# Attention feeding a gated FFN on one core: one small-tile phase per slot, outputs two slots behind, V loaded by ScalarE, nine pairs turned by TensorE

## The chip, the cores and the metric

The kernel runs on one core of a Trainium2 chip. The metric is the time of one execution on the device in microseconds (us); lower is better. The time of the kernel before is the median of three runs. The profile comes from one execution more.

The core has five engines that run side by side, each in its own order: TensorE (PE; its weight loads are listed as PEld), VectorE (DVE), ScalarE (ACT), GpSimd (POOL) and SyncE (SP), which here only starts transfers. TensorE writes only to PSUM. Transfers run on 16 DMA engines that all queues share.

## The reference

`q`, `k` and `v` are 8 x 8 x 576 x 64 (batch, heads, sequence, head dimension), 32-bit floats. Two attentions are added and fed to a gated FFN:

```
q_d, k_d, v_d = means of q, k, v over groups of 4 positions        # 144 positions
out_up    = repeat(softmax(q_d k_d^T / 8) v_d, 4)                  # pooled attention
out_local = softmax(q k^T / 8 where |i - j| < 4) v                 # local attention
x = (out_up + out_local), heads side by side                       # 4608 x 512
out = (relu(x w_gate) * (x w_val)) w_out                           # 512 -> 1536 -> 512
```

## The kernel before

**Pairs and slots.** Two heads of one batch make a pair; there are 32 pairs, and four pairs give 576 rows of `x`. Pair `p` is loaded into `qst`, `kst` and `vst` (three buffers each, `load_qk` L134 and `load_v` L154, all from SP's queue; V takes four transfers), cast to 16 bits (`cast_q`, `cast_k`, `cast_v`), and q and k are turned so that the head dimension is on partitions. Pairs below `N_PE` = 6 are turned by TensorE (`turn_pe`, L215), which also gives the means of q and k in `pd`; the others are turned by two DMA transposes on SP (`turn_dma`, L246), and GpSimd makes their means (`pool_qk`, L258: `ptq`, `pd`, `ptk`, `pd`).

**Attention of a pair.** `scores` (L276) puts on TensorE the means of V (8 matmuls with `p32`, L281), the pooled scores (L292) and the local scores (48 small matmuls, L305), all into the PSUM tile `at` (four banks). `maxima` masks the local scores, takes maxima on VectorE and subtracts on GpSimd (`dd`, L336). `exps` (L343) is on ScalarE: four exponentials of the pooled scores (`e_d`, L348), one of the local ones (`ee`, L356), and the copy of V's means (`vd16`, L357). `weigh` (L359) takes reciprocals on VectorE, scales on GpSimd (`e_d` L365, `pp` L368) and turns the pooled weights by a DMA transpose (`adT`, L374). `turn_p` (L380) turns the local weights on VectorE (`pT`). `sums` (L386) multiplies the weights with V on TensorE (local L391, pooled L401), copies the pooled result to `odx` on ScalarE (L411), and adds both into `xT` on VectorE (L416).

**FFN.** `xT` is cut into nine chunks of 512 tokens. An h unit (`unit_h`, L429) is eight matmuls of 512 columns (L434) into two PSUM buffers, a ReLU on ScalarE (L443) and a product on VectorE (`gT`, L444). A y unit (`unit_y`, L446) is 12 such matmuls (L449) into one PSUM buffer and a copy on ScalarE (L458); `store_y` sends the rows out. Four PSUM buffers serve both kinds. There are 108 h units and 36 y units in the fixed order of `units` (L468): 12 h units of chunk 0, then for each chunk c its 12 h units with a y unit of chunk c - 1 behind the second, fifth, eighth and eleventh.

**Order.** The schedule is written by hand: each engine runs its instructions in the order in which the program issues them, and the build adds the waits between engines. A head (L486 to L526) does the attention of pairs 0 to 3 and loads the weights in pieces from GpSimd's queue. Then each pass of the loop at L530, a slot, does the scores of pair s, some FFN units (`ffn(a[0])` to `ffn(a[3])`; 12 in all in slots 4 to 8, four a slot from slot 9 on), and the sums of pair s - 1. What is left of `units` runs after the loop. Within a slot the order is: loads of pair s + 3, means of pair s + 1 (`pool_qk`), scores and maxima, `ffn(a[0])`, `exps`, `weigh`, `ffn(a[1])`, `sums(s - 1)`, casts of k and `turn_dma` of pair s + 2, `ffn(a[2])`, `turn_p`, `ffn(a[3])`.

Of the kernel before, what the change touches and what calls it, by code (L numbers as in the profile page):

```python
# [16 lines left out]
N_PE = 6  # L17
# [43 lines left out]
def kernel(  # L61
# [39 lines left out]
    qst = many(3, [96, 2, 6, 64], FP32, "qst")  # L101
    kst = many(3, [96, 2, 2, 256], FP32, "kst")
    vst = many(3, [128, 2, 6, 64], FP32, "vst")
# [6 lines left out]
    adT = many(2, [128, 2, 2, 2, 80], FP16, "adT")  # L110
# [7 lines left out]
    vw = many(4, [128, 2, 6, 64], FP16, "vw")  # L118
    vd16 = many(2, [128, 2, 128], FP16, "vd16")
# [8 lines left out]
    pT = many(2, [128, 12, 32], FP16, "pT")  # L128
# [5 lines left out]
    def load_qk(p):  # L134
        base = 2 * p * S * D
        nc.sync.dma_start(qst[p % 3], _dap(q, base, [[D, 96], [S * D, 2], [96 * D, 6], [1, D]]))

        st = kst[p % 3].rearrange("p h c e -> p (h c) e")
# [14 lines left out]

    def load_v(p):  # L154
        st = vst[p % 3].rearrange("p h n d -> p (h n) d")
        for g in range(4):
# [4 lines left out]
            if p == 0 and g == 0:  # L161
                lo = 4
                nc.sync.dma_start(
                    d[0:4, 1:12, :], _dap(v, o + 96 * D, [[D, 4], [96 * D, 11], [1, D]])
                )
            if p == NP - 1 and g == 3:
                hi = 28
                nc.sync.dma_start(
                    d[28:32, 0:11, :], _dap(v, o + 28 * D, [[D, 4], [96 * D, 11], [1, D]])
                )  # L170
            nc.sync.dma_start(
                d[lo:hi], _dap(v, o + lo * D, [[D, hi - lo], [96 * D, 12], [1, D]])
            )

    def load(p):
        load_qk(p)
        load_v(p)
# [20 lines left out]
    def cast_q(p, eng):  # L198
        copy(
            eng,  # L200
            q16[p % 2].rearrange("p j (h d) -> p j h d", d=D),
            qst[p % 3].rearrange("p h j d -> p j h d"),
        )

    def cast_k(p, c, eng):
# [3 lines left out]
            kst[p % 3][0:74, :, c, :].rearrange("p h (r d) -> p r h d", d=D),  # L209
        )  # L210

    def cast_v(p, eng):
        copy(eng, vw[p % 4], vst[p % 3])
# [44 lines left out]
    def pool_qk(p):  # L258
# [4 lines left out]
        )  # L263
        kg = kT[p % 3]
# [10 lines left out]

    def scores(p):  # L276
        qt, kt, pdt, vt = qT[p % 3], kT[p % 3], pd[p % 3], vw[p % 4]
        for n in range(8):
            m = n if n < 6 else n - 2
            x, kc = n % 4, n // 4  # L280
            nc.tensor.matmul(  # L281
                out=at[32 * x : 32 * x + 32, kc, 288:416],
                lhsT=p32,
                rhs=vt[:, :, m, :],
                start=True,
                stop=True,
                tile_position=(0, 32 * x),
            )
        for c in range(2):
            for h in range(2):  # L290
                lo = 64 * h
                nc.tensor.matmul(  # L292
                    out=at[0:72, h, 144 * c : 144 * c + 144],
# [6 lines left out]
        for n in range(6):  # L300
            for g in range(4):
                c, m = n // 3, 4 * (n % 3) + g
                for h in range(2):
                    lo = 64 * h
                    nc.tensor.matmul(  # L305
                        out=at[32 * g : 32 * g + 32, 2 + h, 32 * n : 32 * n + 32],
# [6 lines left out]

    def maxima(p):
        c = col[p % 2]
        nc.vector.tensor_tensor(  # L318
            out=sm[p % 2].rearrange("p (h n) j -> p h (n j)", h=2),
            in0=at[:, 2:4, 0:192],  # L320
            in1=_sap(mask, (0, 128), 0, [[0, 2], [1, 192]]),
            op=ALU.add,
        )
        nc.vector.tensor_reduce(  # L324
            out=c[0:72, 36:40].rearrange("p (h c) -> p h c", h=2),
            in_=at[0:72, 0:2, 0:288].rearrange("p h (c j) -> p h c j", c=2),
# [8 lines left out]
        nc.vector.tensor_reduce(out=c[:, 0:12], in_=sm[p % 2], axis=AX.X, op=ALU.max)  # L335
# [3 lines left out]
            in1=_sap(c, (0, 128), 0, [[1, 12], [0, 32]]),  # L339
# [3 lines left out]
    def exps(p):  # L343
        c = col[p % 2]
        for h in range(2):
            for cc in range(2):
                hc = 2 * h + cc
                nc.scalar.activation(  # L348
                    out=e_d[p % 2][0:72, h, cc, 0:6, 0:24],
                    in_=at[0:72, h, 144 * cc : 144 * cc + 144].rearrange("p (n j) -> p n j", j=24),  # L350
# [4 lines left out]
                )  # L355
        nc.scalar.activation(out=ee[p % 2], in_=dd[p % 2], func=AF.Exp, scale=scale)  # L356
        nc.scalar.copy(out=vd16[p % 2], in_=at[:, 0:2, 288:416])  # L357

    def weigh(p):  # L359
        c = col[p % 2]  # L360
        nc.vector.reciprocal(out=c[0:72, 48:52], in_=c[0:72, 44:48])  # L361
        nc.vector.tensor_reduce(out=c[:, 12:24], in_=ee[p % 2], axis=AX.X, op=ALU.add)  # L362
        nc.vector.reciprocal(out=c[:, 24:36], in_=c[:, 12:24])  # L363
# [3 lines left out]
        )  # L367
        nc.gpsimd.tensor_tensor(  # L368
# [5 lines left out]
        nc.sync.dma_start(  # L374
            adT[p % 2].rearrange("p h c k g -> p (h c k) g"),
            e_d[p % 2].rearrange("p h c n j -> p (h c n j)"),
            transpose=True,
        )

    def turn_p(p):  # L380
        nc.vector.transpose(
            pT[p % 2].rearrange("p n i -> p (n i)"), pp[p % 2].rearrange("p n j -> p (n j)")
        )


    def sums(p):  # L386
        vt, w, vd, ad = vw[p % 4], pT[p % 2], vd16[p % 2], adT[p % 2]
        for n in range(6):
            for h in range(2):
                for g in range(4):  # L390
                    nc.tensor.matmul(  # L391
                        out=at[64 * h : 64 * h + 64, g, 24 * n : 24 * n + 24],
                        lhsT=vt[32 * g : 32 * g + 32, h, n, :],
                        rhs=w[32 * g : 32 * g + 32, 6 * h + n, 0:24],
                        start=True,
                        stop=True,
                        tile_position=(32 * g, 64 * h),
                    )
        for kc in range(2):
            for h in range(2):  # L400
                nc.tensor.matmul(  # L401
                    out=at[64 * h : 64 * h + 64, 3, 144:288],
                    lhsT=vd[:, kc, 64 * h : 64 * h + 64],
                    rhs=ad[:, h, :, kc, 0:72],
                    start=(kc == 0),
                    stop=(kc == 1),
                    tile_position=(0, 64 * h),
                    skip_group_check=True,
                )
# [3 lines left out]
            in_=at[:, 3, 144:288].rearrange("p (n g m) -> p g n m", g=4, n=6),  # L413
        )
        b, kk = p // 4, p % 4
# [4 lines left out]
            in0=at[:, :, 0:144].rearrange("p g (n m f) -> p g n m f", n=6, f=4),  # L420
# [47 lines left out]
    units = []  # L468
    for c in range(NCH):
        for j in range(NJ):  # L470
            units.append(("h", c, j))
            if c and j % 3 == 1:
                units.append(("y", c - 1, j // 3))
# [12 lines left out]
    nc.sync.dma_start(eye, eye_dr)  # L486
    for t in kst[0], vst[0]:
        nc.gpsimd.memset(t, 0.0)
    load(0)
    nc.scalar.dma_start(p32, p32_dr)  # L490
    nc.scalar.dma_start(mask, mask_dr)
    for t in k16 + e_d:
        nc.vector.memset(t, 0.0)
    load(1)
    load(2)
    for t in qT:
        nc.gpsimd.memset(t[:, S:], 0.0)

# [5 lines left out]

    cast_early(0)
    turn_pe(0)
    w_at = {1: [0], 2: [1], 3: [2, 3]}

    for s in range(4):
        cast_early(s + 1)  # L510
        scores(s)
        maxima(s)
        turn_pe(s + 1)
        exps(s)
        weigh(s)
        for i in w_at.get(s, ()):
            load_w(moe_w_gate, wg, 384 * i, 384 * i + 384)
            load_w(moe_w_val, wv, 384 * i, 384 * i + 384)
        load(s + 3)
        turn_p(s)  # L520
        if s:
            sums(s - 1)
    sums(3)
    load_wo(0, 4)
    load_wo(4, 8)
    load_wo(8, 12)  # L526


    per_slot = {4: (1, 1, 1, 0), 5: (1, 1, 1, 0), 6: (1, 1, 0, 0), 7: (1, 1, 0, 0), 8: (1, 1, 0, 0)}
    for s in range(4, NP + 1):  # L530
        a = per_slot.get(s, (1, 1, 1, 1))
        if s == 4:
            cast_q(5, "act")
            cast_k(5, 0, "act")
            cast_k(5, 1, "act")
            cast_v(5, "dve")
        if s + 3 < NP and s > 3:
            load(s + 3)
        store_y()
        if s < NP:  # L540
            if s + 1 < NP and s + 1 >= N_PE:
                pool_qk(s + 1)
            if s + 2 < NP:
                cast_q(s + 2, "act")
            scores(s)
            maxima(s)
        ffn(a[0])
        if s + 1 < N_PE:
            turn_pe(s + 1)
        if s < NP:  # L550
            exps(s)
            if s + 2 < NP:
                cast_v(s + 2, "dve")
            weigh(s)
        ffn(a[1])
        if s > 4:
            sums(s - 1)
        if s + 2 < NP:
            cast_k(s + 2, 0, "act")
            cast_k(s + 2, 1, "act")  # L560
            turn_dma(s + 2)
        ffn(a[2])
        if s < NP:
            turn_p(s)
# [34 lines left out]
```

## Time and profile before

| | |
|---|---|
| median of 3 runs | 440.06 us (439.37 to 444.82) |
| profiled execution, its own time | 442.51 us |
| its span, first to last instruction | 440.8 us |
| TensorE busy | 368.5 us, 84% |
| VectorE, ScalarE, GpSimd busy | 225.9, 220.1, 164.0 us |
| mean granted TensorE clock | 0.969 |
| DMA traffic | 60.94 MB, mean 138 GB/s |

The page of the profile gives each engine's busy time; the span in 40 slices, each digit the busy share in tenths (PEclk is the clock that TensorE was granted, in tenths of full speed); the chain of work that ended last; groups of instructions by line; and the DMA queues. The trace behind it can be listed in order of time (start, length, engine, line, operation, out<-in, and in brackets the idle time before and what ended it) or summed over chosen stretches. SPq and ACTq are the queues from which SP and ScalarE start transfers. Where several instructions of a line are merged, "x48" is their number.

### The profile page before, as it was taken

Reading aid. Unit: us, or ns where it says so; the run is one execution under the profiler, and the core shown is the slowest. Engines: PE = TensorE matmul, PEld = TensorE weight load, DVE = VectorE, ACT = ScalarE, POOL = GpSimd, SP = SyncE. Lnnn points to the kernel's source line nnn. Section 1 sums busy time; section 2 is a strip of 40 time slices with the busy share of each in tenths; the row PEclk is TensorE's granted clock in tenths of the full one; section 3 lists DMA queues with packets and bytes.
Section 4 is the critical chain, followed back from the end, with each engine's and each line's share of the span. In section 5 each row is a group of like instructions: output and inputs, shape, how many; then the busy total and the mean of one; then the engine's idle time right before and its main releaser. Section 6 shows DMA issues by size and latency. Waiting matters only on the chain.

```text
span 440.8 us, 12346 instructions
## 1 busy us (share of the span) xinstructions
PE 368.5 (84%) x5048; PEld 181.1 (41%) x5048; DVE 225.9 (51%) x443; ACT 220.1 (50%) x595; POOL 164.0 (37%) x225
## 2 busy tenths in 40 slices
PE   1634049586789999999999999999979999999996
PEld 1433024243334445444444444444434444444442
DVE  2565024375546666666656666666645632223120
ACT  2464026454546666665666566666645423233321
POOL 2456401444564545544445545555444300000000
PEclk9999996788899999999999999999998999999999
DMA  9999999998999999999998899999654221010012
GB/s 159 158 176 192 180 204 194 153 137 153 154 154 174 175 170 183 188 165 168 164 183 171 184 160 176 186 177 185 134 113 70 42 40 48 26 48 24 25 48 95
DMA packets 165604, 60.94 MB, mean 138 GB/s; under 512 B 144940, under 2 KB 160940, under 8 KB 165548
## 3 DMA queue, kind: packets, MB, share of 16 engines
q1 hardware_dynamic: 159452, 55.34, 72.7%
q0 software_dynamic: 5808, 4.72, 7.6%
q8 instruction: 39, 0.64, 0.6%
q10 hardware_dynamic: 288, 0.11, 0.1%
q14 instruction: 17, 0.14, 0.1%
HBM read 42.08 MB, written 9.44 MB: 117 GB/s over the span
## 4 chain that ended last, share of the span: by engine, by line
PE 54%; ACT 12%; DVE 10%; DMA 10%; POOL 6%; issue 5%; SPq 2%; POOLq 0%; DVEq 0%; ACTq 0%
PE h_ps L434 22%; PE y_ps L449 21%; ACT e_d L348 7%; DMA kst<-in_k_dram 5%; DMA qst<-in_q_dram 4%; DVE col L324 4%; PE at L391 3%; PE at L305 3%; DVE sm L318 3%; ACT ee L356 3%; ACT vd L357 2%; DVE col L331 1%; PE at L401 1%; POOL dd L336 1%; PE at L292 1%
## 5 line engine op out<-in xcount | busy, mean ns | idle before, releaser
L444 DVE TENSOR_TENSOR gT<-r,h_ps 128x512 f16<-128x512 f16 x108 | 73.9, 685 | 131.0 <-PE h_ps L434 126.6
L434 PE MATMUL h_ps<-xT,wg 128*128 128x512 f16 x432 | 117.6, 397 | 0.0
L434 PE MATMUL h_ps<-xT,wv 128*128 128x512 f16 x432 | 115.9, 392 | 0.0
L443 ACT ACTIVATE r<-h_ps 128x512 f16<-128x512 f32 x108 | 64.7, 599 | 74.5 <-PE h_ps L434 74.5
L449 PE MATMUL y_ps<-wo,gT 128*128 128x512 f16 x432 | 100.0, 383 | 0.0
L434 PEld LDWEIGHTS <-wv 128*128 128x128 f16 x432 | 43.6, 101 | 55.2 <-issue 7.4
L434 PEld LDWEIGHTS <-wg 128*128 128x128 f16 x432 | 41.2, 101 | 49.5 <-issue 7.0
L449 PEld LDWEIGHTS <-gT 128*128 128x128 f16 x432 | 40.6, 98 | 48.8 <-issue 1.8
L260 POOL TENSOR_TENSOR ptq<-qT 128x288 f32<-128x288 f16 x26 | 17.3, 666 | 103.5 <-DMA qT<-q 94.7
L458 ACT COPY y_sb<-y_ps 128x512 f32<-128x512 f32 x36 | 21.1, 586 | 69.1 <-PE y_ps L449 69.1
L348 ACT ACTIVATE e_d<-at,col 72x144 f16<-72x144 f32 x128 | 46.6, 371 | 2.5 <-DVE col L331 1.9
L365 POOL TENSOR_TENSOR e_d<-e_d,col 72x576 f16<-72x576 f16 x32 | 36.6, 1142 | 24.9 <-DVE col L361 13.7
L391 PE MATMUL at<-pT,vw 32*64 32x24 f16 x1536 | 17.4, 188 | 31.6 <-ACT vd L357 30.1
L336 POOL TENSOR_TENSOR dd<-sm,col 128x384 f32<-128x384 f32 x32 | 27.0, 842 | 32.1 <-DVE col L335 31.9
L391 PEld LDWEIGHTS <-vw 32*64 32x64 f16 x1536 | 17.5, 108 | 43.0 <-issue 33.6
L192 ACT CAST q<-qst 96x768 f16<-96x768 f32 x32 | 26.3, 823 | 12.9 <-DMA qst<-in_q_dram 12.9
L416 DVE TENSOR_TENSOR xT<-at,odx 128x576 f16<-128x576 f32 x32 | 24.1, 754 | 14.2 <-ACT odx L411 14.2
L192 ACT CAST k<-kst 74x512 f16<-74x512 f32 x54 | 30.7, 618 | 0.0
L362 DVE TENSOR_REDUCE col<-ee 128x12 f32<-128x384 f16 x32 | 17.7, 552 | 19.3 <-ACT ee L356 19.2
L368 POOL TENSOR_TENSOR pp<-ee,col 128x384 f16<-128x384 f16 x32 | 26.5, 829 | 2.4 <-DVE col L363 2.2
L348 ACT ACTIVATION_READ_ACCUMULATOR e_d<-at,col 72x1 f32 x128 | 25.0, 196 | 0.0
L356 ACT ACTIVATE ee<-dd 128x384 f16<-128x384 f32 x32 | 16.6, 520 | 15.4 <-POOL dd L336 15.4
(47 smaller groups left out, 317.1 us busy)
## 6 DMA issues: line engine op xcount, KB each, us to landing
vst<-in_v_dram SPq DMA_DIRECT2D x126, 96.0 KB, 4.8
kst<-in_k_dram SPq DMA_DIRECT2D x30, 320.0 KB, 5.3
qst<-in_q_dram SPq DMA_DIRECT2D x32, 288.0 KB, 4.3
out_dram<-y_sb SPq DMA_DIRECT2D x36, 256.0 KB, 3.5
wg<-in_moe_w_gate_dram POOLq DMA_DIRECT2D x4, 384.0 KB, 7.4
wv<-in_moe_w_val_dram POOLq DMA_DIRECT2D x4, 384.0 KB, 9.9
wo<-in_moe_w_out_dram POOLq DMA_DIRECT2D x3, 512.0 KB, 19.8
adT<-e_d SPq DMA_TRANSPOSE x32, 3.5
```

What stands on the lines that cost most here:

```text
L192: nc.scalar.copy(out=out, in_=in_)
L336: nc.gpsimd.tensor_tensor(out=dd[p % 2], in0=sm[p % 2], in1=_sap(c, (0, 128), 0, [[1, 12], [0, 32]]), op=ALU.subtract,)
L348: nc.scalar.activation(out=e_d[p % 2][0:72, h, cc, 0:6, 0:24], in_=at[0:72, h, 144 * cc : 144 * cc + 144].rearrange("p (n j) -> p n j", j=24),
L356: nc.scalar.activation(out=ee[p % 2], in_=dd[p % 2], func=AF.Exp, scale=scale)
L365: nc.gpsimd.tensor_tensor(out=ed, in0=ed, in1=_sap(c, (0, 72), 48, [[1, 4], [0, 6], [0, 24]]), op=ALU.mult)
L368: nc.gpsimd.tensor_tensor(out=pp[p % 2], in0=ee[p % 2], in1=_sap(c, (0, 128), 24, [[1, 12], [0, 32]]), op=ALU.mult,)
L391: nc.tensor.matmul(out=at[64 * h : 64 * h + 64, g, 24 * n : 24 * n + 24], lhsT=vt[32 * g : 32 * g + 32, h, n, :], rhs=w[32 * g : 32 * g + ...
L416: nc.vector.tensor_tensor(out=xT[:, kk, b * S : (b + 1) * S].rearrange("p (n g m f) -> p g n m f", n=6, g=4, f=4), in0=at[:, :, 0:144].rea ...
L434: nc.tensor.matmul(out=ps, lhsT=w[:, kk, 128 * j : 128 * j + 128], rhs=xT[:, kk, TCH * c : TCH * c + TCH], start=(kk == 0), stop=(kk == 3),)
L443: nc.scalar.activation(out=r, in_=h1, func=AF.Relu)
L444: nc.vector.tensor_tensor(out=gT[c % 2][:, j, :], in0=r, in1=h2, op=ALU.mult)
L449: nc.tensor.matmul(out=ps, lhsT=gT[c % 2][:, j, 128 * t : 128 * t + 128], rhs=wo[:, j, :], start=(j == 0), stop=(j == NJ - 1),)
```

## The change

- **One phase of small matmuls per slot.** `scores` and `sums` are taken apart. A slot s now issues on TensorE, with no FFN unit between: `pooled_v(s)` (means of V), `pooled_out(s - 2)`, `scores(s)`, `local_out(s - 2)`. Outputs, scores and means of V have columns of their own in `at` (`U`, `SCO`, `OD`, `VD1`). `pooled_out` has eight matmuls where there were four; of the eight of `pooled_v`, four have half the width.
- **Outputs two slots behind.** Slots run to s = 33. `evict_od(s - 2)` follows the phase on ScalarE; `add_x(s - 2)` stands on VectorE between the pooled exponentials and the reciprocals.
- **Readers of `at`.** The maxima of the pooled scores come before those of the local ones; V's means are copied in two pieces (`evict_vd`), ahead of `ffn(a[0])`.
- **Means of q and k.** `pool_qk` becomes `pool_q`, between the two weight scalings on GpSimd, and `pool_k`, after `ffn(a[1])`. Both now come after the scores of pair s.
- **Loads.** From slot 5 on V's four transfers are issued from ScalarE's queue, at the start of the slot. The staging tiles have four buffers, `vw` five, `adT`, `vd16` and `pT` three.
- **Nine pairs** are turned by TensorE (`N_PE` = 9).
- **Head.** The first four pairs are loaded before anything else, the small constants come from ScalarE's queue, the memsets are smaller or moved, the weights come in halves of 768 columns, one pair of halves in slot 1 and one in slot 2. Slots 4 to 8 take 10 units instead of 12.

The core of the diff; the renamed parts of `maxima`, `exps`, `weigh` and `sums` keep their operations:

```diff
-N_PE = 6
+N_PE = 9
...
+    U, SCO, OD, VD1 = 0, 144, 336, 432
+
+    def pooled_v(p):
+        for n in range(6):
+            x = n % 4
+            for h in range(2) if n >= 4 else (None,):
+                nc.tensor.matmul(
+                    out=at[32 * x : 32 * x + 32, 3, OD : OD + 128]
+                    if h is None
+                    else at[32 * x : 32 * x + 32, h, VD1 : VD1 + 64],
+                    lhsT=p32,
+                    rhs=vw[p % 5][:, :, n, :] if h is None else vw[p % 5][:, h, n, :],
...
+    def pooled_out(p):
+        vd, ad = vd16[p % 3], adT[p % 3]
+        for kc in range(2):
+            for x in range(4):
+                nc.tensor.matmul(
+                    out=at[32 * x : 32 * x + 32, 2, OD : OD + SD],
+                    lhsT=vd[:, kc, 32 * x : 32 * x + 32],
+                    rhs=ad[:, x // 2, :, kc, 0:72],
...
+    def evict_vd(p, kc):
+        if kc == 0:
+            nc.scalar.copy(out=vd16[p % 3][:, 0, :], in_=at[:, 3, OD : OD + 128])
+        else:
+            nc.scalar.copy(
+                out=vd16[p % 3][0:64, 1, :].rearrange("p (h d) -> p h d", h=2),
+                in_=at[0:64, 0:2, VD1 : VD1 + 64],
+            )
...
-    per_slot = {4: (1, 1, 1, 0), 5: (1, 1, 1, 0), 6: (1, 1, 0, 0), 7: (1, 1, 0, 0), 8: (1, 1, 0, 0)}
-    for s in range(4, NP + 1):
...
+    early = {4: (1, 1, 1, 0), 5: (1, 1, 0, 0), 6: (1, 1, 0, 0), 7: (1, 1, 0, 0), 8: (1, 0, 0, 0)}
+    cast_early(5)
+    for s in range(4, NP + 2):
+        a = early.get(s, (1, 1, 1, 1))
+        now, nxt, two = s < NP, s + 1 < NP, s + 2 < NP
+        if s >= 5 and s + 3 < NP:
+            load_qk(s + 3)
+            load_v(s + 3, nc.scalar)
         store_y()
+        if now:
+            pooled_v(s)
+        if s >= 6:
+            pooled_out(s - 2)
+        if now:
             scores(s)
+        if s >= 6:
+            local_out(s - 2)
+            evict_od(s - 2)
+        if now:
+            pooled_max(s)
+            evict_vd(s, 0)
+            evict_vd(s, 1)
+            local_max(s)
+            local_sub(s)
         ffn(a[0])
+        if now:
+            pooled_exp(s)
+        if s >= 6:
+            add_x(s - 2)
+        if now:
+            local_exp(s)
+            pooled_weights(s)
+            if nxt and s + 1 >= N_PE:
+                pool_q(s + 1)
+            local_weights(s)
+            turn_pooled(s)
+        if two:
+            cast_v(s + 2, "dve")
         ffn(a[1])
+        if nxt:
+            if s + 1 < N_PE:
+                turn_pe(s + 1)
+            else:
+                pool_k(s + 1)
+        if two:
+            cast_q(s + 2, "act")
+        if now:
+            turn_local(s)
+        ffn(a[2])
+        if two:
+            cast_k(s + 2, 0, "act")
+            cast_k(s + 2, 1, "act")
+            if s + 2 >= N_PE:
+                turn_dma(s + 2)
         ffn(a[3])
```

More of the change, by code (lines that the diff above doesn't have):

```diff
@@ L152, in load_qk, with load_v @@
                 )
-    def load_v(p):
-        st = vst[p % 3].rearrange("p h n d -> p (h n) d")
+    def load_v(p, queue):
+        st = vst[p % 4].rearrange("p h n d -> p (h n) d")
         for g in range(4):
@@ L263, in pool_qk, with pool_k @@
         )
+    def pool_k(p):
         kg = kT[p % 3]
@@ L367, in weigh, with turn_pooled, local_weights @@
         )
+    def turn_pooled(p):
+        nc.sync.dma_start(
+            adT[p % 3].rearrange("p h c k g -> p (h c k) g"),
+            e_d[p % 2].rearrange("p h c n j -> p (h c n j)"),
+            transpose=True,
+        )
+    def local_weights(p):
+        c = col[p % 2]
+        nc.vector.tensor_reduce(out=c[:, 12:24], in_=ee[p % 2], axis=AX.X, op=ALU.add)
+        nc.vector.reciprocal(out=c[:, 24:36], in_=c[:, 12:24])
         nc.gpsimd.tensor_tensor(
@@ L373, in weigh, with turn_local, evict_od, add_x @@
         )
[L374 to L377, printed above, removed]
-        )
[L380 to L409, printed above, removed]
+    def turn_local(p):
+        nc.vector.transpose(
+            pT[p % 3].rearrange("p n i -> p (n i)"), pp[p % 2].rearrange("p n j -> p (n j)")
+        )
+    def evict_od(p):
         nc.scalar.copy(
             out=odx[p % 2].rearrange("p (g n m) -> p g n m", g=4, n=6),
-            in_=at[:, 3, 144:288].rearrange("p (n g m) -> p g n m", g=4, n=6),
+            in_=at[:, 2, OD : OD + SD].rearrange("p (n g m) -> p g n m", g=4, n=6),
         )
+    def add_x(p):
         b, kk = p // 4, p % 4
@@ L466, in store_y @@
         stores.clear()
-    units = []
-    for c in range(NCH):
+    units = [("h", 0, j) for j in range(NJ)]
+    for c in range(1, NCH):
+        late = [("y", c - 1, t) for t in range(4)]
         for j in range(NJ):
             units.append(("h", c, j))
-            if c and j % 3 == 1:
-                units.append(("y", c - 1, j // 3))
+            if j % 3 == 1 and late:
+                units.append(late.pop(0))
     units += [("y", NCH - 1, t) for t in range(4)]
@@ L483, in ffn @@
                 store_y()
[L486 to L489, printed above, removed]
+    nc.scalar.dma_start(eye, eye_dr)
     nc.scalar.dma_start(p32, p32_dr)
     nc.scalar.dma_start(mask, mask_dr)
[L492 to L495, printed above, removed]
+    nc.vector.memset(kst[0][0:32, 0, 0, :], 0.0)
+    nc.vector.memset(vst[0][0:32, 0, 0, :], 0.0)
+    for p in range(4):
+        load_qk(p)
+        load_v(p, nc.sync)
+    for t in k16:
+        nc.gpsimd.memset(t[64:80], 0.0)
+    for t in e_d:
+        nc.gpsimd.memset(t, 0.0)
     for t in qT:
         nc.gpsimd.memset(t[:, S:], 0.0)
+    for t in vd16:
+        nc.gpsimd.memset(t[64:128, 1, :], 0.0)
     def cast_early(p):
@@ L503, in cast_early @@
         cast_v(p, "pool")
+    w_at = {
+        1: [(moe_w_gate, wg, 0), (moe_w_val, wv, 0)],
+        2: [(moe_w_gate, wg, 1), (moe_w_val, wv, 1)],
+    }
     cast_early(0)
     turn_pe(0)
-    w_at = {1: [0], 2: [1], 3: [2, 3]}
     for s in range(4):
-        cast_early(s + 1)
-        scores(s)
-        maxima(s)
-        turn_pe(s + 1)
[L514 to L520, printed above, removed]
-        if s:
-            sums(s - 1)
```

170 lines of the change are left out of this document (88 added, 82 removed).

## The prediction

> **What bounds the kernel now.** I read the 40 slices first, then the stretches of 10 us, then the timeline of one steady slot, then the clock. The slices say that TensorE is full from 130 us on; before that it is half empty.
>
> ```profile
> span 440.8 us, 12346 instructions
> ...
> PE   1634049586789999999999999999979999999996
> ...
> PEclk9999996788899999999999999999998999999999
> ```
>
> A steady slot is one pass of the loop at L530; this one takes 9.97 us (from one y unit at 217.13 to the next at 227.12). Its timeline (start, length, engine, line, what):
>
> ```profile
> 217.13 2.76 PE L449 MATMUL y_ps<-wo,gT 128*128 128x512 f16 x12
> ...
> 222.06 0.67 POOL L260 TENSOR_TENSOR ptq<-qT 128x288 f32<-128x288 f16 x1 [4.07 <-DMA qT<-q]
> ...
> 222.81 0.42 POOL L261 TENSOR_TENSOR pd<-ptq 128x144 f16<-128x144 f32 x1
> 223.10 3.09 SPq L171 DMA_DIRECT2D vst<-in_v_dram  x4
> ...
> 223.35 0.73 POOL L265 TENSOR_TENSOR ptk<-kT 128x288 f32<-128x288 f16 x1
> ...
> 224.16 0.49 POOL L268 TENSOR_TENSOR pd<-ptk 128x144 f16<-128x144 f32 x1
> ...
> 226.05 1.14 POOL L365 TENSOR_TENSOR e_d<-e_d,col 72x576 f16<-72x576 f16 x1 [0.58 <-DVE col L361]
> ...
> 226.41 0.53 PE L391 MATMUL at<-pT,vw 32*64 32x24 f16 x48 [0.24 <-ACT vd L357]
> ...
> 227.15 0.83 POOL L368 TENSOR_TENSOR pp<-ee,col 128x384 f16<-128x384 f16 x1
> ```
>
> The reader is to see two things. TensorE's only wait is before L391: its h units are issued by 226.11, and the sums start at 226.41, once ScalarE's L357 (226.00, 0.36 long) has read `at`. And GpSimd does the pooling of the next pair (L260 to L268) early in the slot, while the scores' exponentials are not ready, so the next pair's `pd` exists at 224.65, 7 us before its scores at 231.77. That slack is what the change spends.
>
> TensorE's slot: y 2.70 (to the h unit at 219.89), three h units at 1.73 = 5.19, scores 0.97, the wait and its handover 0.33, sums 0.78: 9.97.
>
> The clock, last (stretch, length, busy time of PE, PEld, DVE, ACT, POOL, granted clock, DMA share, GB/s):
>
> ```profile
> 104.13:107.54 3.41, 1.89 (x113) 1.50 (x113) 2.62 (x5) 2.85 (x7) 1.42 (x2) 1.00 0.75 126
> 107.54:110.95 3.41, 3.41 (x9) 1.18 (x8) 1.84 (x4) 1.62 (x8) 0.66 (x1) 0.50 0.65 88
> 326.00:329.40 3.40, 0.80 (x4) 0.29 (x3) 0.63 (x3) 0.98 (x4) 3.32 (x5) 1.00 0.23 78
> 329.40:332.81 3.41, 3.25 (x58) 1.55 (x58) 2.53 (x5) 1.92 (x5) 1.22 (x2) 0.50 0.67 66
> ```
>
> A stretch of 3.41 us that holds almost no 512-column matmuls is followed by 3.41 us at clock 0.50. In the first pair, TensorE was idle or on small tiles from 102.16 to 107.42. Where that lasted 3.1 us or more (93.72 to 96.84, 102.16, 112.73, 326.80) the half clock followed each time; after 122.74 to 125.51 (2.8 us) and 194.94 to 196.8 it did not.
>
> **The change part by part.**
>
> *One small-tile phase.* It removes the wait, 0.33. `pooled_v` is 8 matmuls, four of them of half width: 0.18 to 0.23, now 0.23. `pooled_out` has 8 matmuls of 32 columns of weights where L401 has 4 of 64 in 0.25: between 0.25 and 0.50; I take 0.26, by L281, whose 8 matmuls of that shape take 0.23 for 128 columns. The phase is 0.23 + 0.26 + 0.24 (L292) + 0.56 (L305) + 0.53 (L391) = 1.82, and TensorE's own slot 2.70 + 5.19 + 1.82 = 9.7. This would gain 0.27 a slot, if nothing else set the slot.
>
> *What is late next.* Something else does. Count the units: slots 4 to 8 now take 10, slot 9 takes h 10 and 11 of chunk 0 and h 0 and 1 of chunk 1, and so from slot 10 on `ffn(a[0])` is always the y unit (16 units a chunk, 4 a slot). `pooled_exp` stands behind `ffn(a[0])` on ScalarE, so it waits for the y copy; before, the first unit was an h unit, whose ReLU needs only its first four matmuls. Behind the exponentials, VectorE runs `add_x` of pair s-2, then the reciprocal; GpSimd then scales `e_d`, then `pool_q(s + 1)`, then `pp`, then `pool_k(s + 1)`; and `scores(s + 1)` needs `pool_k(s + 1)`. In the built program these are real waits: the readers of `at` also take turns between ScalarE and VectorE (pooled output, maxima, `vd16`, masked scores, exponentials, `add_x`). Round the loop, from the end of the small-tile phase:
>
> - y 2.70; its copy 0.59 + 0.04
> - four exponentials 1.55 (L348, 224.14 to 225.69); `add_x` 0.76 (L416); reciprocal and handover 0.24 (L361)
> - GpSimd: `e_d` 1.14 (L365), `pool_q` 1.17 (222.06 to 223.23), `pp` 0.83, `pool_k` 1.30 (223.35 to 224.65) = 4.44
> - scores and sums 0.24 + 0.56 + 0.53 = 1.33
>
> Sum 11.65, less 0.05 for an overlap on ScalarE: 11.6 us. The five other readers of `at` (odx 0.28, maxima 0.74, vd 0.36, sm 0.56, with handovers 2.1) run under y and its copy, 3.3; without that cover they would be in the loop.
>
> *V loads on ScalarE.* SP gives up 3.09 of some 9 us a slot; nothing waits for SP, so that is worth 0. ScalarE gains four issues, 0.49 to 0.77 each by L171 on SP (ScalarE's own two, of other shapes, took 0.37 and 0.46). Behind them are the copy of the pooled output and all that takes turns on `at`. The program also makes the fourth wait for the slot's `qT` transpose on SP: issued after `e_d` and `adT` (1.20), 8.1 after the phase's end, landing 3.0 to 3.6 later, so the fourth load is out at 11.6 to 12.2, and `vd16` done 1.5 later: 1.5 to 2.1 into the y unit of 2.7. I take 0; a transpose that lands 1.5 us later costs 0.9 a slot.
>
> *Nine pairs turned by TensorE.* Pairs 6 to 8 lose two DMA transposes and 2.5 us of GpSimd each and gain 28 matmuls (some 0.9), 1.04 on ScalarE, 0.48 on VectorE, in slots 5 to 7. *Head:* four pairs loaded ahead instead of three, weights in halves, smaller memsets. In the page's slices DMA is 0.9 or more busy until 100 us, and the same bytes must arrive. Slot 10 began at 129.93 with 16 units done; now 14 are due, two h units less: 129.9 - 3.5 = 126.4, say 127. Bounds: if slots 7 and 8 (10.6 and 10.0) go like slot 6 (7.3) and the rest gains 3, minus 9; one pair (992 KB) more ahead of slot 4 at 170 GB/s is 5.8, with three turns' evictions 3 more, plus 9.
>
> *The clock.* In a slot of 11.6, TensorE is idle 11.6 - 9.7 = 1.9, then or before that on small tiles 1.82: 3.7 us without wide matmuls, above the 3.1 that was followed by half clock each time. The stretch from 326.00 held 2.6 us without wide matmuls and was followed by half clock, that from 100.71 to 104.13 held 1.97 (from 102.16 on) and was not; I put the limit between them, at 2.3. Cut by fixed stretches of 3.41, the 3.7 us fall into two parts x and 3.7 - x, both under 2.3 only for x from 1.4 to 2.3: 0.9 / 3.41 = 26% of positions. So in 74% half clock follows. It then meets the y unit, which is on the loop: half clock from 0.5 us in leaves 2.2 us of 2.59 done at 3.9 and ends it at 4.3, 1.65 later. So 0.74 x 1.65 = 1.2: slots of 12.8 (11.6 without, 13.25 with it in each).
>
> *After slot 31.* 14 + 22 x 4 units are done, 28 h and 14 y are left: 28 x 1.73 + 14 x 2.59 = 84.7; two phases of outputs 1.6; the last copy and store 3.6 (437.22 to 440.8): 90.
>
> **Sum.** 127 + 22 x 12.8 + 90 = 498.6 of span. The profiled execution took 442.51 for a span of 440.8; the median of the runs shown is 440.06, 0.7 below that span. So 498 us.
>
> A rule speaks against my clock term: the Trainium skill (TensorE: Matmul & The Clock Gate, section "HAM oscillation — how this bites in real kernels") warns of idle gaps over some 3.4 us, and 1.9 is under it. The trace differs: the half clock at 107.54 came after gaps of 2.33 and 1.16 us with small matmuls between. By that rule the sum would be the second case below.
>
> **The rivals.**
>
> - *The clock stays up* while the loop holds: 127 + 22 x 11.6 + 90 - 0.7 = 471. For it: L391-like matmuls may count as work. Against: 104.13 to 107.54 had 1.89 us of PE busy time and was followed by 0.50.
> - *ScalarE's queue sets the slot*: transposes land 1.5 us late, the V issue holds the copies back 0.9 more: 498 + 22 x 0.9 = 518. For it: SP's landings spread from 2.9 to 3.6. Against: SP has less to issue.
> - *TensorE sets the slot, as the change says*: 9.7 a slot, 127 + 213.4 + 90 - 0.7 = 430, 421 to 439 with the head's bounds: faster or the same. It decides if the way from the y unit's end to `pool_k`'s end takes less than TensorE's own 5.19 + 0.49 = 5.7 us; the rows give 7.6. For it: only that GpSimd's pooling has slack now. Against: each wait is in the program.
>
> **How the numbers follow.** Forecast 0.58, clock up 0.20, ScalarE's queue 0.12, TensorE's bound 0.10, of which 0.06 is more than 2% below 440.06 (under 431.3) and 0.04 is within. 2% is about what a measurement of this kernel can tell from no change. Slower 0.90, same 0.04, faster 0.06. The likeliest case alone runs from 485 to 512; the range takes in the second with the head's gain (471 - 8) and the third: 463 to 517.
>
> **What would show it.** Slots of 12 to 13 us from 130 us on; TensorE waiting before the pooled scores for GpSimd's `pd`, about 2 us a slot; GpSimd's `e_d` waiting for VectorE's reciprocal behind `add_x`; the y copy ending just ahead of the exponentials; clock 0.5 in many slices from 130 to 380 us; slot 32 starting near 409 us. Wrong: slots under 10 us, no wait for `pd`, a clock row of nines, or a wait of ScalarE's copies for DMA that decides the slot.

## The result and the profile after

The changed kernel takes **504.56 us** (median of 4 runs, 502.55 to 517.31) where the kernel before, run beside it, takes 439.72 (439.18 to 444.82): a ratio of **1.143, 95% interval 1.132 to 1.154**. The profiled execution is the longest of the four, 517.31 us for a span of 515.3; ratios here leave out disturbed executions, so a ratio can differ a little from the quotient of two medians.

The page of the changed kernel (PE's busy share and its granted clock, in tenths, in 40 slices):

```profile
span 515.3 us, 12727 instructions
...
PE   2250209884988888888888888888888889999996
...
PEclk9999999885988898888888888888887889999999
```

TensorE, full from 130 us on before, is now mostly at eight tenths from slice 12 to slice 33, its clock mostly at eight tenths with it, and slices 4 to 6 hold a hole. A slot is counted here from the start of its pooled scores to the next one's. Slot 10 starts at 136.2, slot 32's outputs at 425.1. Between them a slot takes 11.75 us in 2 of 21 cases and 12.9 or more in 18, most often 13.44.

The timeline of such a slot (start, length, engine, line, what, idle time before and what ended it):

```profile
255.07 4.45 PE L481 MATMUL y_ps<-wo,gT 128*128 128x512 f16 x12
...
259.56 0.59 ACT L490 COPY y_sb<-y_ps 128x512 f32<-128x512 f32 x1 [2.81 <-PE y_ps L481]
...
260.04 0.38 ACT L387 ACTIVATE e_d<-at,col 72x144 f16<-72x144 f32 x1
...
261.62 0.76 DVE L448 TENSOR_TENSOR xT<-at,odx 128x576 f16<-128x576 f32 x1 [3.70 <-ACT e_d L387]
...
262.29 0.16 DVE L410 RECIPROCAL col<-col 72x4 f32<-72x4 f32 x1
...
262.59 1.14 POOL L412 TENSOR_TENSOR e_d<-e_d,col 72x576 f16<-72x576 f16 x1 [3.76 <-ACT r L475]
...
263.69 0.98 POOL L256 TENSOR_TENSOR ptq<-qT 128x288 f32<-128x288 f16 x1
...
264.75 0.43 POOL L257 TENSOR_TENSOR pd<-ptq 128x144 f16<-128x144 f32 x1
...
265.13 0.83 POOL L427 TENSOR_TENSOR pp<-ee,col 128x384 f16<-128x384 f16 x1
...
265.92 0.74 POOL L263 TENSOR_TENSOR ptk<-kT 128x288 f32<-128x288 f16 x1
...
266.74 0.49 POOL L266 TENSOR_TENSOR pd<-ptk 128x144 f16<-128x144 f32 x1
267.28 0.32 PE L313 MATMUL at<-pd 64*72 64x144 f16 x4 [2.16 <-POOL pd L266]
...
268.52 1.87 PE L481 MATMUL y_ps<-wo,gT 128*128 128x512 f16 x5
```

Read it downwards: each line starts about where the one above ends (three more exponentials follow L387, until 261.6). The y unit, its copy, the exponentials, `add_x`, the reciprocal, four pieces of work on GpSimd, and only then the scores of the next pair, for which TensorE has waited 2.16 us. (Before L412 the trace names a ReLU as the last releaser, by its end at about the same time; what L412 reads are the exponentials and the reciprocal, and it starts 0.14 after the latter.) The y unit at the top took 4.45 instead of 2.76. Two stretches of 3.41 us of this pass say why (length, busy PE, PEld, DVE, ACT, POOL, granted clock, DMA share, GB/s):

```profile
255.40:258.81 3.41, 3.41 (x10) 1.21 (x8) 2.03 (x4) 0.52 (x3) 0.81 (x1) 0.51 1.05 245
...
265.63:269.04 3.41, 1.76 (x103) 1.34 (x103) 1.75 (x3) 0.27 (x1) 1.52 (x3) 1.00 0.92 187
```

The second holds the wait and the small matmuls; half clock follows it from 269.0 on, and the first is such a half clock, lying on the y unit.

### The profile page after: what moved, and what is told of

Its sections match the earlier page's. It is cut to its first block, busy times and chain, and to the rows that moved or that the text cites. A ratio compares the mean times of both kernels' runs of the same rounds, so it can differ in the third digit from the quotient of the medians.

```text
span 515.3 us, 12727 instructions
## 1 busy us (share of the span) xinstructions
PE 393.0 (76%) x5260; PEld 191.8 (37%) x5260; DVE 235.6 (46%) x445; ACT 221.0 (43%) x631; POOL 163.0 (32%) x215
## 4 chain that ended last, share of the span: by engine, by line
PE 44%; DVE 12%; POOL 11%; ACT 11%; DMA 10%; issue 8%; SPq 3%; ACTq 1%; DVEq 0%; POOLq 0%
PE y_ps L481 23%; PE h_ps L466 12%; ACT e_d L387 7%; DMA adT<-e_d 5%; DVE xT L448 4%; POOL pp L427 3%; DVE gT L476 3%; POOL ptk L263 3%; PE at L326 3%; PE at L339 3%; DMA vst<-in_v_dram 2%; ACT y_sb L490 2%; SPq L141 2%; POOL pd L266 2%; DVE col L425 2%
## 5 line engine op out<-in xcount | busy, mean ns | idle before, releaser
L481 PE MATMUL y_ps<-wo,gT 128*128 128x512 f16 x432 | 129.0, 464 | 0.0
L466 PE MATMUL h_ps<-xT,wg 128*128 128x512 f16 x432 | 115.2, 388 | 4.3 <-DVE xT L448 2.7
L476 DVE TENSOR_TENSOR gT<-r,h_ps 128x512 f16<-128x512 f16 x108 | 70.8, 672 | 57.0 <-PE h_ps L466 57.0
L481 PEld LDWEIGHTS <-gT 128*128 128x128 f16 x432 | 47.6, 115 | 67.8 <-issue 39.1
L441 ACT CAST odx<-at 128x144 f16<-128x144 f32 x32 | 8.9, 279 | 133.8 <-PE at L339 87.1
L412 POOL TENSOR_TENSOR e_d<-e_d,col 72x576 f16<-72x576 f16 x32 | 36.6, 1144 | 71.9 <-ACT r L475 68.3
L387 ACT ACTIVATE e_d<-at,col 72x144 f16<-72x144 f32 x128 | 46.6, 373 | 15.1 <-DVE sm L365 14.6
L352 DVE TENSOR_REDUCE col<-at 72x4 f32<-72x576 f32 x32 | 24.1, 752 | 51.6 <-ACT odx L441 46.8
L313 PE MATMUL at<-pd 64*72 64x144 f16 x128 | 11.1, 250 | 47.0 <-POOL pd L266 46.4
L298 PE MATMUL at<-adT,vd 128*32 128x144 f16 x256 | 11.7, 243 | 43.4 <-DMA adT<-e_d 39.9
L435 DVE STREAM_TRANSPOSE pT<-pp 128x384 f16<-128x384 f16 x32 | 18.4, 576 | 33.2 <-POOL pp L427 33.2
L190 DVE CAST vw<-vst 128x768 f16<-128x768 f32 x26 | 28.5, 1096 | 0.0
```

Of the source, the lines that this page charges most:

```text
L190: nc.vector.tensor_copy(out=out, in_=in_)
L387: nc.scalar.activation(out=e_d[p % 2][0:72, h, cc, 0:6, 0:24], in_=at[0:72, h, lo : lo + SD].rearrange("p (n j) -> p n j", j=24), func=AF.Exp,
L412: nc.gpsimd.tensor_tensor(out=ed, in0=ed, in1=_sap(c, (0, 72), 48, [[1, 4], [0, 6], [0, 24]]), op=ALU.mult)
L466: nc.tensor.matmul(out=ps, lhsT=w[:, kk, 128 * j : 128 * j + 128], rhs=xT[:, kk, TCH * c : TCH * c + TCH], start=(kk == 0), stop=(kk == 3),)
L476: nc.vector.tensor_tensor(out=gT[c % 2][:, j, :], in0=r, in1=h2, op=ALU.mult)
L481: nc.tensor.matmul(out=ps, lhsT=gT[c % 2][:, j, 128 * t : 128 * t + 128], rhs=wo[:, j, :], start=(j == 0), stop=(j == NJ - 1),)
```

## The experiments

The kernel before was run again beside each group of these runs, and ratios are to that. L numbers of kernels with moved lines are their own. Means of slots are over slots 10 to 30, from the start of one slot's pooled scores to the next.

**1. The changed kernel again.**

> The changed kernel once more, for a profile near its median of 504.6 us: the profiled execution took 517.31, and its slot 4 began only at 77.8 us. If that late start belongs to that execution alone, slot 4 begins near 60 to 66 us here and the slots from 12 on are the same 13.4 us (11.75 where the clock stayed up).

516.47 us in one profiled execution. Slots of 13.4 and 11.75 again. Slot 4 starts at 79.8, not at 60 to 66, so the late start was not of one execution alone. Its size varies: run 5's kernel is the same up to slot 10, and there slot 4 starts at 66.5.

**2. Pooling early, as in the kernel before.**

```diff
+        if nxt and s + 1 >= N_PE:
+            pool_q(s + 1)
+            pool_k(s + 1)
         if now:
             pooled_v(s)
...
-            if nxt and s + 1 >= N_PE:
-                pool_q(s + 1)
             local_weights(s)
...
-            else:
-                pool_k(s + 1)
```

> The changed kernel with pool_q and pool_k of pair s + 1 moved to the start of slot s, as before the change. GpSimd's loop as the only limit: scores no longer wait for pd, the slot falls from 13.4 to TensorE's 9.7, and the time to 127 + 22 x 9.7 + 90 = about 430 us. ScalarE's queue as a second loop right behind it (fourth V load waits for the qT transpose, which waits for e_d; then odx 0.28, maxima 0.74, vd 0.45, y copy 0.6, exponentials 1.55, add_x 0.76, reciprocal 0.24, e_d 1.14, adT 1.2, landing of qT 3 to 3.6, V issue 0.5): 10.5 to 11.1 us a slot, 450 to 470 us. Neither: no change from 504.

484.62 us (1.0974, 1.0928 to 1.102): 20 us better, yet worse than either theory had it. Slots swing between 9.5 and 15.8, about 12 on average.

**3. V from SP's queue.**

```diff
-            load_v(s + 3, nc.scalar)
+            load_v(s + 3, nc.sync)
```

> The changed kernel with V's loads issued from SP again. GpSimd's loop: the slots stay at 13.4 (11.6 where the clock stays up), the time within 12 us of 504. ScalarE's queue as the limit: slots of 9.7 to 10, 430 to 440 us.

507.08 us (1.1464, 1.1386 to 1.1542): no change, slots of 13.44 and 11.75. In 200 to 330 us TensorE waits as often and as long for GpSimd as in the changed kernel, so V's issues on ScalarE do not set the slot there.

**4. Both edits.**

> Both edits of the two runs before together. If there are two loops, one behind the other, only this one reaches TensorE's own 9.7 to 10.2 us a slot and 430 to 440 us, with no half clock after 130 us. If GpSimd's loop is the only one, this equals the kernel with the early pools alone. If TensorE's phase itself is what is slow, it stays above 470.

452.13 us (1.0218, 1.016 to 1.0277), slots of 10.5 in the middle and 10.7 on average, no half clock between 130 and 330 us. The time is above the 430 to 440 that was expected: TensorE's own sum is not reached. Still, the one word that was worth nothing in run 3 is worth 32 us once the loop through GpSimd is gone. The waits from 200 to 330 us (engine, line, waited for: us in total, times, longest), run 2 and then run 4:

```profile
DVE col L352 <- ACT odx L441: 33.4, 11, 5.0
...
ACT odx L441 <- PE h_ps L466: 15.9, 3, 5.9
...
ACT odx L441 <- DMA qT<-q: 11.6, 3, 4.4
```

```profile
POOL ptq L256 <- DMA qT<-q: 38.4, 10, 4.9
...
ACT ee L397 <- POOL dd L374: 10.7, 12, 1.7
```

In run 2 ScalarE's first copy of the slot (`odx`) waits up to 5.9 us, and the maxima on VectorE behind it. In run 4 that is gone; what is left is GpSimd waiting for the `qT` transpose at the start of the slot, with the subtraction `dd` behind that.

**5. The wait filled with wide matmuls.**

```diff
+        if now and s >= 10:
+            fill = fpsum.tile([128, TCH], FP32, name="fill_ps", tag="f")
+            for i in range(5):
+                nc.tensor.matmul(
+                    out=fill, lhsT=wg[:, i % 4, 0:128], rhs=wv[:, i % 4, 0:512],
+                    start=True, stop=True,
+                )
         if now:
             scores(s)
```

> The changed kernel with five matmuls of 512 columns on the weights (into a PSUM buffer that nobody reads) ahead of the pooled scores of slots 10 to 31, where TensorE otherwise waits some 2 us for GpSimd's pd. This leaves the loop through GpSimd as it is and takes away only the stretch without wide matmuls. Theory (the half clock is a consequence of the wait and costs 1.65 us a slot by way of the y unit): almost no half clock between 140 and 400 us, slots of 11.75 instead of 13.4, 504 - 22 x 1.65 = 468 us, 465 to 475. Rival (the half clock meets units that are not on the loop, or comes anyway): slots of 13.2 or more, 500 us or more.

487.94 us in the median, with runs from 481.9 to 494.96; ratio 1.0856 (1.0806 to 1.0907). From the clock row and the timeline of one slot:

```profile
PEclk9999999776999999999999999999999999999999
```

```profile
196.32 1.25 PE L601 MATMUL fill_ps<-wv,wg 128*128 128x512 f16 x5
198.54 0.32 PE L313 MATMUL at<-pd 64*72 64x144 f16 x4 [0.97 <-POOL pd L266]
```

Extra work of 1.25 us a slot makes the kernel faster: no half clock between 122 and 480 us, and 14 of 21 slots from slot 10 on take 11.74 or 11.75. The mechanism is as the theory said; the total missed its range of 465 to 475. In ratios the clock was worth 1.143 - 1.0856 = 0.057, of 440 us 25 us, where the expectation, taking 13.4 for every slot, had 36. The traces agree: slots 10 to 30 fall from 13.24 to 12.06 on average, 24.7 us in all, since some were at 11.75 before and some still take 12 to 15.

**6. The exponentials ahead of the y unit.**

```diff
-        ffn(a[0])
         if now:
             pooled_exp(s)
+        ffn(a[0])
```

> The changed kernel with the four pooled exponentials on ScalarE ahead of ffn(a[0]), one line moved. Theory (the loop runs through the y unit, its copy, the exponentials, add_x, the reciprocal and GpSimd): the exponentials no longer wait for the y unit and its copy (2.70 + 0.63), but for the readers of at that were hidden under them (2.1 of waits, ending some 2.2 us after the phase), so the loop loses about 1.1 us: 11.75 becomes 10.6; TensorE's stretch without wide matmuls becomes 0.9 + 1.8 = 2.7, so the half clock comes in some slots only, and it falls on a y unit that is no longer on the loop: slots of 10.6 to 11.3, 504 - 22 x 2.5 = 449, 442 to 470 us. Rival (the y unit is not in the loop, GpSimd's four pieces and the V issue on ScalarE alone set the slot): less than 10 us gained, 495 or more.

482.19 us (1.0753, 1.0703 to 1.0804). The gain is larger than the rival allows and smaller than the 442 to 470 that was expected. Several slots are 10.75 (expected 10.6), the mean of slots 10 to 30 is 11.5, above the range, the half clock still comes six times between 140 and 345 us, and slot 10 starts at 133.7. The y unit was in the loop; taking it out leaves GpSimd's pieces in it.

**7. All three edits of runs 2, 3 and 6.**

> The changed kernel with the pooling of the next pair at the start of the slot, all of V's loads from SP, and the pooled exponentials ahead of ffn(a[0]). With the first two edits it took 452 us, slots of 10.5, where the h units wait for ReLUs and the exponentials stand behind a y copy. Theory: with the exponentials first the rest of the loop is under TensorE's own 9.7, slots of 9.7 to 10.0: 452 - 22 x 0.65 = 438 us, 430 to 443. Rival (another loop, through GpSimd's subtraction dd behind the pooling of k that waits for its transpose, sets 10.5): 448 to 455.

456.92 us (1.0284, 1.0219 to 1.0349): the rival. Slots of 10.5, as in run 4. With the pooling at the start of the slot, `dd` stands behind a wait for a transpose (from 200 to 330 us GpSimd waits 29.8 us for `qT`, and the local exponentials 15.3 us for `dd`), and the exponentials' place hardly matters. Run 11 tests this.

**8. The same, weights in quarters.**

```diff
         2: [(moe_w_gate, wg, 1), (moe_w_val, wv, 1)],
+        3: [(moe_w_gate, wg, 2), (moe_w_val, wv, 2), (moe_w_gate, wg, 3), (moe_w_val, wv, 3)],
     }
...
-            load_w(src, dst, 768 * i, 768 * i + 768)
+            load_w(src, dst, 384 * i, 384 * i + 384)
```

> The same three edits, and w_gate and w_val in quarters of 384 columns as in the kernel before: one pair of quarters in slot 1, one in slot 2, two in slot 3 (instead of halves in slots 1 and 2). Theory (the head's slot 4 starts at 70 to 80 us instead of 60 because 3 MB of weights are queued by 39 us and pair 2's and 3's adT transposes and SP's issues stand behind them): slot 4 starts at 60 to 66, 5 to 10 us less than the kernel with the same three edits. Rival (four pairs loaded ahead instead of three make the lateness): slot 4 unchanged, the time within 2 us.

437.2 us (0.9843, 0.9806 to 0.988), 19.7 less than run 7, twice the upper end of what was expected. Slot 4 starts at 56.8 instead of 72.8, slot 10 at 116.4 instead of 132.5, and the four runs agree within 1.3 us where those of run 7 lay 5.3 apart.

**9. The kernel before, with late pooling alone.**

```diff
-            if s + 1 < NP and s + 1 >= N_PE:
-                pool_qk(s + 1)
...
             out=ed, in0=ed, in1=_sap(c, (0, 72), 48, [[1, 4], [0, 6], [0, 24]]), op=ALU.mult
         )
+        if nxt:
+            pool_qk(p + 1)
...
         ffn(a[1])
+        if s + 1 < NP and s + 1 >= N_PE:
+            pool_k(s + 1)
```

(`pool_qk` here keeps only the half for q, `pool_k` has the rest.)

> The kernel before with one part of the change: the means of q and k of the next pair no longer at the start of the slot, but pool_q between the two scalings on GpSimd and pool_k behind ffn(a[1]). Theory (late pooling costs only where the exponentials stand behind a y unit): here two h units follow the scores and the y unit comes third, so e_d is scaled at 226.05 and pd would be ready 4.44 us later, at 230.5, before the scores at 231.8: the kernel before's time within 1%. Rival (late pooling alone makes the loop): slots of 10.5 or more, 452 us or more.

429.65 us, **0.9724 (0.9693 to 0.9755)**: a gain that neither theory had. Slots 10 to 30 take 209.5 us, 9.97 each; in the kernel before they take 216.1, with one slot of 13.84. SP ahead of that slot of the kernel before, and GpSimd in it:

```profile
313.04 4.47 SPq L149 DMA_DIRECT2D kst<-in_k_dram  x2
...
325.17 0.67 POOL L260 TENSOR_TENSOR ptq<-qT 128x288 f32<-128x288 f16 x1 [6.54 <-DMA qT<-q]
...
327.86 0.83 POOL L336 TENSOR_TENSOR dd<-sm,col 128x384 f32<-128x384 f32 x1
```

The scores are there from 323.2 on, but `dd`, the local exponentials and `vd16` behind them stand behind a pooling that waits for a late transpose. The transpose is late because the last pair's K comes in two more pieces (L149), and SP holds the second until the first has landed, at 317.1. That is what early pooling costs, and what late pooling saves: 6.6 us in these slots, 3.8 of them in this one. The other half of the gain, 6.7 us, lies ahead of slot 10, which starts at 123.5 instead of 130.2. Of it 4.4 us lie ahead of slot 4 (55.5 instead of 59.9), where the edit has not yet changed any instruction; one trace of each kernel does not tell where these come from.

**10. The changed kernel with weights in quarters alone.**

> The changed kernel with w_gate and w_val in quarters as in the kernel before (one pair of quarters in slot 1, one in slot 2, two in slot 3). Theory: the head's adT transposes and SP's issues no longer stand behind 3 MB of weights, slot 4 starts at 56 to 60 instead of 66 to 80, and some 10 to 15 us of this last to the end: 490 to 495 us, slots of 11.75 to 13.4 as before. Rival (the later slots take the gain back, since the loop starts when the FFN units of slots 4 to 9 are done): 500 or more.

495.47 us (1.1162, 1.1086 to 1.1237), 9 less (12 by the ratios). The slots are much as before, 12.94 on average beside 13.24; slot 4 starts at 55.3 and slot 10 at 120.5. SP's queue, the changed kernel and then this one:

```profile
35.69 7.00 SPq L417 DMA_TRANSPOSE adT<-e_d  x1
42.74 0.59 SPq L136 DMA_DIRECT2D qst<-in_q_dram  x1
43.43 10.67 SPq L141 DMA_DIRECT2D kst<-in_k_dram  x1
54.14 8.99 SPq L171 DMA_DIRECT2D vst<-in_v_dram  x4
63.24 2.33 SPq L417 DMA_TRANSPOSE adT<-e_d  x1
```

```profile
35.26 2.46 SPq L417 DMA_TRANSPOSE adT<-e_d  x1
...
44.57 3.88 SPq L417 DMA_TRANSPOSE adT<-e_d  x1
```

With 3 MB of weights issued by 39.9 us, one K load takes SP 10.67 us to issue, and the weights of pair 3's pooled attention are turned at 63.2 instead of 44.6.

**11. Run 8 with the pooling behind the subtraction.**

```diff
-        if nxt and s + 1 >= N_PE:
-            pool_q(s + 1)
-            pool_k(s + 1)
         if now:
             pooled_v(s)
...
             local_sub(s)
+        if nxt and s + 1 >= N_PE:
+            pool_q(s + 1)
+            pool_k(s + 1)
         if now:
             pooled_exp(s)
```

> The kernel with three edits and weights in quarters (437 us, slots of 10.25), with the next pair's pooling on GpSimd moved from the start of the slot to behind the subtraction dd, still ahead of the scalings. Theory (dd stands behind the pooling of k, which waits for its DMA transpose, and ee, pp, pT and the h units' ReLUs follow dd): slots of 9.7 to 10.0, 425 to 433 us. Rival (PSUM buffers freed late by ReLUs behind the exponentials set 10.25): 435 to 440.

**423.99 us (0.9584, 0.9553 to 0.9615)**: the best of all, slots of 9.45 to 9.6 with a few of 10 to 11, 9.85 on average.

**12. The same, V back on ScalarE's queue.**

> The fastest kernel so far (424 us: next pair's pooling behind dd, exponentials first, weights in quarters, V from SP) with V's four loads of a slot back on ScalarE's queue, one word changed. Theory (a second loop, hidden in the changed kernel behind the one through GpSimd: the later two V issues wait on ScalarE for the slot's transposes on SP, and the copies of the next slot's small-tile phase stand behind them, until the y unit waits for vd and the exponentials): slots of 11.5 to 12.5 instead of 9.7, the y copy following vd at once, 424 + 22 x 2.3 = 475 us, 455 to 490. Rival (V from ScalarE's queue costs nothing, as the prediction said): 424, 420 to 430.

493.33 us (1.1139, 1.1085 to 1.1194): 69 us for one word (`nc.scalar` in place of `nc.sync`), more than the theory's 51. Slots take 12.94 on average and swing between 9.5 and 17.5. SP's and ScalarE's queues and ScalarE's and TensorE's work in one slot:

```profile
237.77 1.21 SPq L243 DMA_TRANSPOSE qT<-q  x1
239.08 1.88 SPq L248 DMA_TRANSPOSE kT<-k  x1
```

```profile
239.14 0.33 ACTq L171 DMA_DIRECT2D vst<-in_v_dram  x1
...
241.49 0.32 ACTq L171 DMA_DIRECT2D vst<-in_v_dram  x1
241.91 0.28 ACT L441 CAST odx<-at 128x144 f16<-128x144 f32 x1 [5.06 <-DMA vst<-in_v_dram]
```

```profile
246.12 1.02 PE L466 MATMUL h_ps<-xT,wv 128*128 128x512 f16 x4 [2.85 <-ACT y_sb L490]
```

ScalarE is idle for 5.06 us ahead of its first copy. Each of the last two V loads waits on a semaphore that a transpose of this slot sets when it has landed: the third for `adT` (239.1), the fourth for `qT` (241.5). These waits are the program's, as the prediction said for the fourth; the issues themselves take 0.3 us. `vd`, the exponentials and the y copy follow the first copy, and TensorE, whose PSUM buffers that copy frees, waits 2.85. `qT` stands on SP behind `adT`, which waits for `e_d`, and `e_d` for those exponentials: a second loop, through ScalarE's queue and the landings of SP's transposes.

## Why the prediction was right, and where it was not

**The sum, term by term.** In the profiled execution: start of slot 10 136.2 (predicted 127), 22 slots of (425.1 - 136.2) / 22 = 13.13 (12.8), the rest 515.3 - 425.1 = 90.2 (90). The 16.7 us by which its span exceeds 498.6 are 9.2 of head, 7.3 of slots and 0.2 of rest. The runs without a profile were 13 to 15 us shorter than this one, within 1.4% of the forecast; which of the two terms was smaller there no trace shows. Run 5's kernel, the same up to slot 10, starts that slot at 128.0. With that start and the same rest, their spans of some 502.5 leave 12.9 a slot (an estimate), close to both terms of the sum.

**The loop: right.** 11.6 was predicted, 11.74 measured where the clock stays up (run 5), and the timeline after has every link in the order in which it was written. Runs 2 to 4 and 6 show that it is the cause: run 6 takes the y unit out of it and gains, run 4 takes the pooling out of it and, with V on SP, gains 52 us. Two links were off: the first sum of `pool_q` took 0.98 instead of 0.67, and the phase of small matmuls was shorter than 1.82: without a wait, in run 11, it takes 1.59 (192.63 to 194.22), and the slot reaches 9.45, under the 9.7 of TensorE's own sum.

**The clock: right in size, low in frequency.** A half clock on the y unit costs 13.44 - 11.75 = 1.69 (predicted 1.65; its own figures, 4.3 - 2.59, give 1.71). It was to come in 74% of slots; there were 18 half clocks in 21 slots. The estimate took the slot's position against the fixed stretches as random. It isn't: a slot of 13.44 is nearly four stretches of 3.41 (13.64), so the position hardly moves, and the half clocks at 149.5, 163.2 and 176.9 are 13.7 apart. Run 5 shows the half clock to be a consequence of the wait. TensorE was idle for only 2.16 us, and the small-tile matmuls next to the wait did not keep the clock up: the stretch from 265.63 holds 1.24 us of them and, at its end, 0.52 of the next y unit, and half clock follows. The rival in which the clock stays up, 471, is out. The Trainium skill (TensorE: Matmul & The Clock Gate, section "HAM oscillation — how this bites in real kernels") warns of idle gaps over some 3.4 us; by that alone none should have come, and the trace differs.

**The head: its cost put on the wrong part.** 136.2 is 127 + 9.2, just over the upper bound of 9. Counted from the first small matmul, as the prediction counted 129.93, slot 10 starts at 134.8, within it. The price was put on one more pair loaded ahead; runs 8 and 10 show that it is the weights in halves. In the four kernels with quarters, with the same four pairs, slot 4 starts at 55.3 to 57.5, in the eight traces with halves at 66.5 to 82.6; in run 10 slot 10 starts at 120.5. That 127 came out so near is in part luck: with quarters slot 10 starts 6 to 11 us before that, and the halves, which the sum did not price, put this back. The step that failed is "weights in halves" counted only as bytes: the bytes are the same, but pair 2's and pair 3's `adT` and SP's loads stand behind them.

**V on ScalarE at 0: right here, for a reason that was too thin.** The cover named, the y unit, holds while the loop through GpSimd is longer (run 3). From SP the same loads save 32 us when that loop is gone (run 2 against 4) and 69 in the best kernel (run 11 against 12). The rival "ScalarE's queue" had the mechanism and the wrong condition: it doesn't add to the slot, it waits behind the first loop. (Its landings of 2.9 to 3.6 were too narrow: in the steady slots of the kernel before, where the trace tells, `qT` lands 2.6 to 4.2 us after its issue.)

**TensorE's bound.** It does not hold in the changed kernel, as the rows said. It nearly holds in run 11, where GpSimd's pooling fits between `dd` and the scalings: TensorE is idle for 0.2 us a slot there, for 2.1 in the changed kernel.

**What the prediction had wrong about the kernel before.** Its early pooling was read as slack that costs nothing, TensorE's 9.97 as the slot. Run 9 is 12 us faster without it. Of these, its traces place 6.6 us in the steady slots: where `qT` lands late, `dd` is late, and with it the next phase. Whether all of the rest is the early pooling's is not shown. The wait of 4.07 for `qT` stood in the lines shown, and was passed over because GpSimd had nothing else to do in that slot.

**Where the change's idea stands.** One phase of small matmuls, outputs two slots behind and nine pairs turned by TensorE are not what made the kernel slow. With the pooling moved, V on SP, the exponentials first and the weights in quarters they make 423.99, beside 429.65 for the kernel before with late pooling alone. Little of that lead is the one phase itself: slots 10 to 30 take 206.8 us against 209.5, where the forecast gain of 0.27 a slot would be 5.7. Slot 10 starts 7.4 us earlier, with two FFN units fewer done, and what follows slot 31 takes 4.9 longer. Whether the old order with the pooling behind `dd` would do as well was not run.

## What to carry to other kernels

When work is moved on an engine that has slack, write down the whole way round to the next pass's first instruction, not the engine's busy time: here GpSimd, busy for 32% of the span, set a slot of 11.75 us together with what stood before it in the loop on other engines. Take away one loop and measure the next one behind it: an edit that is worth nothing alone (V's queue, 0 us) can be worth 32 or 69 us beside another. And look for the waits that the build adds: here a load on one queue waited for the landing of a transpose on another. On an engine that works in order, put what waits for a transfer behind what the present pass needs, and keep small, urgent transfers ahead of large ones.

## What was not expected of the hardware

- **VectorE and GpSimd slow each other down.** In the kernel before, a cast of V on VectorE (L194) that overlaps no GpSimd work takes 0.55 us (four casts), and most of the others, which overlap `dd` by 0.3 to 0.4 us, take 0.71 to 0.81. In the changed kernel the cast (L190) overlaps the scaling of `e_d` and the first pooling sum on GpSimd (L256) in 22 slots and takes 1.04 to 1.35; L256 takes 0.98 in all 22, and 0.66 in the one slot without that overlap. Not every pair does this: in run 11 casts beside the pooling's second sums take 0.56.
- **Wide matmuls into a buffer that nobody reads pay for themselves**: 1.25 us of them a slot took away half clocks that cost 1.69 each (run 5).
- **Issuing was slow while the weights were in flight**: a K load that takes SP 0.6 us to issue in a steady slot took 10.67 then, and the `adT` transpose, 1.2 in a steady slot, took 7.00. That the queued weights are the cause is argued from run 10, where with quarters the same two took 1.82 and 2.46.
